# Attention and a routed expert layer on one core: GpSimd and SyncE put under a written order

## The chip, the cores and the metric

The kernel runs on one core of one Trainium2 chip. The metric is the device time of one execution in microseconds. TensorE (PE), VectorE (DVE), ScalarE (ACT), GpSimd (POOL) and SyncE (SP) each work through a queue of their own, in order; an instruction waits at the head of its queue until its semaphores are reached, and everything behind it waits with it. The program on every queue is fixed when the kernel is built.

## The reference

Softmax with one extra unit in the denominator, and then a layer of experts in which each token takes the one expert whose embedding is nearest in angle:

```python
scores = scale * q @ k.T                       # q, k, v: (8, 12, 448, 64)
m = scores.max(-1); e = exp(scores - m)
attn_out = (e / (e.sum(-1) + exp(-m) + 1e-9)) @ v
x = attn_out.transpose(0, 2, 1, 3).reshape(3584, 768)
logits = normed(x) @ normed(expert_emb).T / tau          # 8 experts
expert_idx = logits.argmax(1); gate_w = softmax(logits)[expert_idx]
out[mask_e] = gate_w * (relu(x[mask_e] @ w1[e]) @ w2[e]) # 768 -> 1024 -> 768
```

## The kernel before, in words

There are 8 batches. The 12 heads of a batch are taken in pairs, so a batch has `NP` = 6 groups, 48 in all, and each group has `NSLOT` = 8 slots. `pipeline` (L644) gives each step a position in slots, sorts the positions and runs the steps in that order. With `g` the group and 8g its first slot:

- `load_qk(n)` and `load_v(n)` (L156, L181) load queries, keys and values for two groups (g = 2n and 2n+1): nine and three DMAs, issued by SyncE, into three sets of buffers. A set is free once `front_q`, `front_k` (for q and k) or `front_v` and `sum_v` (for v) have used the loads three earlier.
- `front_q`, `front_k` transpose on TensorE. `front_v` (L250) is four GpSimd copies (L255 twice, L259, L263) that put v into one of two tiles `vab`; it must wait until TensorE has finished with the same tile two groups earlier.
- `scores` is a product on TensorE, an exponential on ScalarE and a subtraction of 1 on VectorE. `attend` and `attend_rest` (L302, L315) multiply by v and a column block of ones, so that the denominators come with the result; ScalarE copies it to `nb` and issues a small DMA of the denominators into `den`.
- `sum_v` (L194) adds up v over the rows in four GpSimd instructions (L198, L199, L202 twice), for the part of the sum that the subtraction of 1 took away; `sum_v_rows` (VectorE) and `sum_v_mm` (L218, TensorE, once a batch) finish it.
- `recip` (L337) makes reciprocals of the denominators on VectorE (tile `rc`, L346), and one GpSimd instruction (L348) spreads them into `rt`. `normalise` (L354) multiplies `rt` by a selection matrix on TensorE (L359) and then scales `nb` on VectorE (L364). There is one `rt` for two groups, so two `normalise` use each.
- The router of a batch (`router_mm` to `router_gate`) finds the expert of each token and the commonest expert of the batch. GpSimd takes a square root in it (L406), loads the number of the commonest expert into a register (L472) and fetches that expert's weights in seven pieces (`fetch`, `w_piece`, L485; three of w1, four of w2). `keep_xb` (L494) scatters the batch's x to DRAM by an indirect DMA from GpSimd (L503), which a later pass for the other experts reads if there are any.
- The expert's own work is cut into 15 chunks (`moe_chunks`, L557) that fill slots of the six groups from 6b+14 on: eight `moe_h`, then seven outputs y in the order (0,0), (0,1), the rest rows, (1,0), (1,1), (2,0), (2,1), at slots 1 and 5 of group 6b+17, 1, 5 and 7 of 6b+18, 1 and 5 of 6b+19. VectorE writes y into one of three tiles of the pool `yp`, and SyncE stores it (L568, L574). So the fourth y needs the store of the first to have landed, and the seventh, y(2,1), needs that of y(1,0).

What order the queues have: the pipeline is built under a manual schedule for TensorE alone, which keeps the order in which `pipeline` ran the steps. On the other engines the framework's scheduler orders the instructions at build time from its own estimates, held back in a few places by explicit "behind" edges. `fetch` holds one, behind the last `front_v`:

```python
    with tc.manual_schedule(engines={mybir.EngineType.PE}):
        pipeline(n)
```

Of the kernel before, what the change touches and what calls it, by code (L numbers as in the profile page):

```python
# [21 lines left out]
NP = H // 2  # L22
# [314 lines left out]
def recip(k, gg):  # L337

    nc = k.nc
    den, rc = k.den.pop(gg), k.rc[gg % 2]  # L340
    n = 2 * GP * CH
    i = nc.vector.tensor_scalar_add(den[:], den[:], float(S) + 1.0 + 1e-9)
    behind(k, i, k.last)
    nc.vector.reciprocal(out=den[:], in_=den[:])
    nc.vector.tensor_copy(out=rc[0:n, :], in_=den[:])
    nc.vector.tensor_tensor(out=rc[64 : 64 + n, :], in0=den[:], in1=rc[0:n, :].bitcast(F32), op=ALU.subtract)  # L346
    rt = k.rtp.tile([128, CH, CN], F32R, name="rt", tag="rt")
    nc.gpsimd.tensor_tensor(  # L348
        out=rt[:], in0=rc[:].bitcast(F32).unsqueeze(1).broadcast_to([128, CH, CN]), in1=k.chunk[:], op=ALU.mult
    )  # L350
    k.rts[gg] = rt
# [46 lines left out]
def router_tok(k, b):  # L398
# [7 lines left out]
    nc.gpsimd.tensor_tensor(out=nrm[:], in0=nrm[:], in1=k.half[:], op=ALU.pow)  # L406
# [12 lines left out]
    k.ohb[b], k.lg[b] = ohb, (l, nrm)  # L419

# [35 lines left out]
def router_pick(k, b):  # L456

    nc, p = k.nc, k.rp
    cp = k.work.tile([128, 512], F32, name="work", tag="work")
    nc.tensor.matmul(cp[:, 0 : 4 * E], lhsT=k.ones_b[:], rhs=k.ohb[b][:].rearrange("p t e -> p (t e)"),  # L460
                     start=True, stop=True)
    cnt = k.cnt_all[:, b, :]
    nc.vector.reduce_sum(out=cnt, in_=cp[:, 0 : 4 * E].rearrange("p (t e) -> p e t", e=E), axis=AX.X)
    mx = p.tile([128, 8], F32, name="mx", tag="mx")
    k.mx[b] = mx[:, 0:1]
    nc.vector.max(mx[:], cnt)
    nc.vector.max_index(k.idx_all[:, b, :], mx[:], cnt)
    idf = p.tile([128, 1], F32, name="idf", tag="idf")
    nc.vector.tensor_copy(out=idf[:], in_=k.idx_all[:, b, 0:1])
    oh0 = k.oh0_all[:, b, :]  # L470
    nc.vector.tensor_scalar(out=oh0, in0=k.iota[:], scalar1=idf[:, 0:1], scalar2=None, op0=ALU.is_equal)
    e0 = nc.values_load(k.idx_all[0:1, b, 0:1].bitcast(I32), engines=(mybir.EngineType.Pool,),  # L472
                        min_val=0, max_val=E - 1)
    k.e0[b], k.wts[b] = e0, ([], [])


def w_piece(k, e0, i):
# [7 lines left out]
    return w, k.nc.gpsimd.dma_start(w[:], src)  # L485


def fetch(k, b, i):
    w, inst = w_piece(k, k.e0[b], i)
    behind(k, inst, k.last_v)  # L490
    k.wts[b][i // 3 > 0].append(w)


def keep_xb(k, b):  # L494
# [7 lines left out]
    )  # L502
    nc.gpsimd.indirect_dma_start(  # L503
# [53 lines left out]
def moe_chunks(k, b):  # L557
# [21 lines left out]
def other_experts(k):  # L579
# [13 lines left out]
    with tc.If(any_ > 0):  # L593
# [6 lines left out]
        with tc.For_i(0, B * E, 1) as i:  # L600
# [3 lines left out]
            with tc.If(n > 0):  # L604
# [6 lines left out]
                w = [w_piece(k, e, j)[0] for j in range(7)]  # L611
# [32 lines left out]
def pipeline(k):  # L644
# [7 lines left out]
    put(3, lambda: build_late_consts(k))  # L652
    put(12, lambda: prep_expert_emb(k, k.emb, k.tau))
    put(5 * NSLOT, lambda: prep_expert_emb_t(k))
    for n in range(NG * B):
        put(max(-NSLOT, (n * GP - 6) * NSLOT + 4.5), lambda n=n: load_qk(k, n))
        put(max(-NSLOT, (n * GP - 6) * NSLOT + 7.5), lambda n=n: load_v(k, n))
        put(max(0, n * GP - 2) * NSLOT + 1.2, lambda n=n: sum_v(k, n))
        put(max(0, n * GP - 2) * NSLOT + 6.2, lambda n=n: sum_v_rows(k, n))
    for b in range(B):  # L660
        put((b * NP + 3) * NSLOT + 4.5, lambda b=b: sum_v_mm(k, b))
    for g in range(G):
# [3 lines left out]
        put(s - 1, lambda g=g: front_v(k, g))  # L666
# [37 lines left out]
def kernel(  # L704
# [86 lines left out]
```

## Time and profile before

| | before |
|---|---|
| median of 2 runs | 482.13 us (481.28 to 482.98) |
| the profiled execution | 485.81 us |
| its span, first to last instruction | 483.9 us |
| mean granted TensorE clock in it | 0.926 |

The span is what the engines' rows cover; the remaining 1.9 us of the profiled execution lie around it. The granted clock is a share of 2.4 GHz, and in a stretch it is either 1.0 or 0.5 (1.2 GHz). In the views below, times are microseconds from the start of the span unless ns is written; "x6" counts merged instructions; what stands in square brackets is the idle time of that engine just before, and what ended it.

### The profile page before, as it was taken

Reading aid. Unit: us, or ns where it says so; the run is one execution under the profiler, and the core shown is the slowest. Engines: PE = TensorE matmul, PEld = TensorE weight load, DVE = VectorE, ACT = ScalarE, POOL = GpSimd, SP = SyncE. Lnnn points to the kernel's source line nnn. Section 1 sums busy time; section 2 is a strip of 40 time slices with the busy share of each in tenths; the row PEclk is TensorE's granted clock in tenths of the full one; section 3 lists DMA queues with packets and bytes.
Section 4 is the critical chain, followed back from the end, with each engine's and each line's share of the span. In section 5 each row is a group of like instructions: output and inputs, shape, how many; then the busy total and the mean of one; then the engine's idle time right before and its main releaser. Section 6 shows DMA issues by size and latency. Waiting matters only on the chain.

```text
span 483.9 us, 7759 instructions
## 1 busy us (share of the span) xinstructions
PE 416.8 (86%) x2392; PEld 253.3 (52%) x2392; DVE 328.4 (68%) x827; ACT 274.5 (57%) x419; POOL 213.6 (44%) x412
## 2 busy tenths in 40 slices
PE   7587878877996979969898799969996999988986
PEld 5355545454564655636465454636564565654443
DVE  4458897948595666957669666867786686885213
ACT  2555776647684557836577456845785476824030
POOL 3764455446454435526245345545455353421400
PEclk9868999769998889979899899989999799999999
DMA  8762455559957786767978599577957572686893
GB/s 178 181 143 73 117 114 116 113 91 186 178 99 151 142 188 149 136 131 141 214 132 157 109 211 206 103 166 139 241 115 156 113 154 39 98 203 106 166 210 118
DMA packets 135373, 69.97 MB, mean 145 GB/s; under 512 B 101528, under 2 KB 129176, under 8 KB 135328
## 3 DMA queue, kind: packets, MB, share of 16 engines
q1 hardware_dynamic: 115392, 43.63, 36.8%
q0 software_dynamic: 16384, 25.17, 32.6%
q10 hardware_dynamic: 3552, 0.63, 0.9%
q8 instruction: 20, 0.33, 0.3%
q14 instruction: 25, 0.20, 0.1%
HBM read 83.39 MB, written 16.52 MB: 206 GB/s over the span
## 4 chain that ended last, share of the span: by engine, by line
PE 44%; DVE 16%; POOL 14%; issue 12%; DMA 6%; ACT 2%; POOLq 0%; SPq 0%; DVEq 0%; ACTq 0%
PE big L302 9%; PE work L515 8%; PE work L530 5%; DVE x L364 5%; DMA out_dram<-y 5%; PE big L277 5%; PE work L389 4%; DVE em L284 3%; PE work L545 3%; PE work L359 3%; POOL rt L348 3%; PE big L315 2%; POOL vs L202 2%; POOL vs L199 2%; PE work L231 2%
## 5 line engine op out<-in xcount | busy, mean ns | idle before, releaser
L282 ACT ACTIVATE e<-big 128x896 f32<-128x896 f32 x144 | 128.3, 921 | 65.3 <-DVE x L364 26.2
L284 DVE TENSOR_SCALAR em<-e 128x896 fp32r<-128x896 f32 x144 | 97.9, 680 | 39.0 <-ACT e L282 37.4
L255 POOL TENSOR_SCALAR vab<-vld 128x192 fp32r<-128x192 f32 x96 | 34.7, 374 | 139.2 <-PE big L302 109.9
L515 PE MATMUL work<-xb,w 128*128 128x448 bf16 x384 | 83.1, 356 | 3.7 <-DVE y L534 1.6
L364 DVE SCALAR_TENSOR_TENSOR x<-nb,sv,work 64x448 f32<-64x448 f32 x96 | 65.0, 677 | 28.3 <-PE work L359 25.9
L302 PE MATMUL big<-em,vab 128*128 128x448 f32 x288 | 77.4, 409 | 6.5 <-ACT e L282 5.5
L322 ACT COPY nb<-big 128x896 f32<-128x896 f32 x48 | 43.5, 907 | 61.0 <-PE big L315 60.9
L530 PE MATMUL work<-w,h 128*128 128x384 bf16 x384 | 68.7, 327 | 0.0
L302 PEld LDWEIGHTS big<-em,vab 128*128 128x128 f32 x288 | 59.0, 210 | 15.3 <-ACT e L282 7.5
L277 PE MATMUL big<-qt,kt 64*128 64x448 f32 x288 | 55.0, 434 | 5.4 <-ACT kt L246 2.4
L359 PE MATMUL work<-rt,sel 128*128 128x448 f32 x48 | 25.7, 535 | 38.7 <-POOL rt L348 30.2
L515 PEld LDWEIGHTS <-w 128*128 128x128 bf16 x384 | 35.1, 99 | 39.3 <-issue 12.0
L520 ACT ACTIVATE h<-work 128x448 bf16<-128x448 f32 x64 | 34.8, 544 | 33.8 <-PE work L515 33.6
L534 DVE TENSOR_SCALAR y<-work,g 128x384 f32<-128x384 f32 x48 | 29.2, 610 | 33.9 <-DMA out_dram<-y 16.2
L530 PEld LDWEIGHTS <-h 128*128 128x128 bf16 x384 | 35.9, 98 | 25.9 <-issue 5.3
L485 POOL DMA_DIRECT2D w<-in_moe_w_dram x56 | 43.4, 779 | 13.7 <-PE work L530 5.8
L234 DVE CAST qt<-work 128x448 fp32r<-128x448 f32 x48 | 29.9, 623 | 20.3 <-PE work L232 19.6
L277 PEld LDWEIGHTS big<-qt,kt 64*128 64x128 f32 x288 | 26.0, 205 | 20.4 <-issue 9.0
L359 PEld LDWEIGHTS work<-rt,sel 128*128 128x128 f32 x48 | 10.3, 214 | 49.2 <-POOL rt L348 35.9
L198 POOL TENSOR_TENSOR vs<-vld 128x256 f32<-128x256 f32 x24 | 18.1, 754 | 39.0 <-issue 33.2
L202 POOL TENSOR_TENSOR vs<-vs,vrest 64x128 f32<-64x128 f32 x48 | 26.6, 554 | 18.5 <-DMA xb_dram<-xb,keep_i 15.4
L246 ACT CAST kt<-work 128x512 fp32r<-128x512 f32 x48 | 28.2, 588 | 7.1 <-PE work L244 5.5
(117 smaller groups left out, 611.6 us busy)
## 6 DMA issues: line engine op xcount, KB each, us to landing
w<-in_moe_w_dram POOLq DMA_DIRECT2D x24, 512.0 KB, 6.9
w<-in_moe_w_dram POOLq DMA_DIRECT2D x32, 384.0 KB, 6.8
qm<-in_q_dram SPq DMA_DIRECT2D x72, 128.0 KB
vld<-in_v_dram SPq DMA_DIRECT2D x24, 384.0 KB
out_dram<-y SPq DMA_DIRECT2D x48, 192.0 KB
km<-in_k_dram SPq DMA_DIRECT2D x69, 128.0 KB
qrest<-in_q_dram SPq DMA_DIRECT2D x24, 64.0 KB
vrest<-in_v_dram SPq DMA_DIRECT2D x48, 32.0 KB
```

Of the source, the lines that this page charges most:

```text
L202: nc.gpsimd.tensor_tensor(out=vs[r, h::2, :], in0=vs[r, h::2, :], in1=t.vr[r, :, :], op=ALU.add)
L277: nc.tensor.matmul(ps[:, h, 0:S], lhsT=kt[64 * h : 64 * h + 64, 128 * j : 128 * j + 128], rhs=qt[64 * h : 64 * h + 64, :], start=True, sto ...
L282: k.last_e = nc.scalar.activation(e[:], ps[:, :, 0:S], ACT.Exp, scale=scale)
L284: k.last = nc.vector.tensor_scalar_sub(em[:], e[:], 1.0)
L302: nc.tensor.matmul(ps[:, h, 0:S], lhsT=va[:, j, 2 * h : 2 * h + 2, :], rhs=k.ems[g, j][:, h, :], start=(j == 0), stop=False,)
L322: nc.scalar.copy(out=nb[:, i, :, :], in_=ps[:, :, 0:S])
L359: nc.tensor.matmul(ps[:, 0:S], lhsT=k.sel[:, g % GP, :], rhs=rt[:].rearrange("p c n -> p (c n)"), start=True, stop=True)
L364: nc.vector.scalar_tensor_tensor(out=x[r, :], in0=nb[0:64, g % GP, h, :], scalar=k.sv[b][:, 2 * c + h : 2 * c + h + 1], in1=ps[r, 0:S], op ...
L485: return w, k.nc.gpsimd.dma_start(w[:], src)
L515: nc.tensor.matmul(ps[:, 0:S], lhsT=w1[c // 2][:, c % 2, 128 * f : 128 * f + 128], rhs=xb[:, c, :], start=(c == 0), stop=(c == NP - 1),)
L520: nc.scalar.activation(h[:], ps[:, 0:S], ACT.Relu)
L530: nc.tensor.matmul(ps[:, 0:SM], lhsT=hs[f][:, 128 * t : 128 * t + 128], rhs=w2[f // 2][:, f % 2, SM * n : SM * n + SM], start=(f == 0), st ...
```

## The change

GpSimd and SyncE join the manual schedule, so that their queues, too, run in the order of `pipeline`'s positions. With that, the steps are cut where they belong to different engines and get positions of their own:

- `recip` keeps the VectorE part; the spread of `rt` becomes `spread`, at slot 2 of the group whose slot 6.5 holds `normalise`.
- `front_v(g)` moves from slot 8g-1 to 8g-3.8. `sum_v` moves from slot 1.2 to 5 of its group; `sum_v_rows` from 6.2 to 8.
- `load_qk` moves from 4.5 to 5 and `load_v` from 7.5 to 7 of the same group.
- `fetch` moves from slot 7.7 to 4.3 of its group and loses its "behind" edge. `keep_xb` is cut: its two VectorE instructions (`keep_rows`) at `router_mm` + 13, the scatter at +16 instead of +14. The square root (`router_pow`) and the register load (`router_index`) are steps of their own at +5.6 and +11 (they ran with `router_tok` at +4 and `router_pick` at +7.6).
- The store of a y stands 2.5 slots behind its chunk.
- `build_late_consts` moves from 3 to 4.6. `prep_expert_emb`, whose position 12 is unchanged, holds one SyncE load (L129) and one GpSimd square root (L134).

```diff
@@ recip
+def spread(k, gg):
+    nc, rc = k.nc, k.rc[gg % 2]
     rt = k.rtp.tile([128, CH, CN], F32R, name="rt", tag="rt")
     nc.gpsimd.tensor_tensor(
...
@@ router_tok
-    nc.gpsimd.tensor_tensor(out=nrm[:], in0=nrm[:], in1=k.half[:], op=ALU.pow)
+def router_pow(k, b):
+    nrm = k.lg[b][1]
+    k.nc.gpsimd.tensor_tensor(out=nrm[:], in0=nrm[:], in1=k.half[:], op=ALU.pow)
@@ router_pick
+def router_index(k, b):
+    k.e0[b] = k.nc.values_load(k.idx_all[0:1, b, 0:1].bitcast(I32), engines=(mybir.EngineType.Pool,),
+                               min_val=0, max_val=E - 1)
+    k.wts[b] = ([], [])
@@ fetch
-    w, inst = w_piece(k, k.e0[b], i)
-    behind(k, inst, k.last_v)
+    w = w_piece(k, k.e0[b], i)
@@ moe_chunks
     def y(t, n):
         def run():
             yt = moe_y(k, hs, k.wts[b][1], k.g0[b], t, n)
-            nc.sync.dma_start(out_main(k.out, b * S, t, n), yt[:])
+            return lambda: nc.sync.dma_start(out_main(k.out, b * S, t, n), yt[:])
         return run
@@ pipeline
-    put(3, lambda: build_late_consts(k))
+    put(4.6, lambda: build_late_consts(k))
...
-        put(max(-NSLOT, (n * GP - 6) * NSLOT + 4.5), lambda n=n: load_qk(k, n))
-        put(max(-NSLOT, (n * GP - 6) * NSLOT + 7.5), lambda n=n: load_v(k, n))
-        put(max(0, n * GP - 2) * NSLOT + 1.2, lambda n=n: sum_v(k, n))
-        put(max(0, n * GP - 2) * NSLOT + 6.2, lambda n=n: sum_v_rows(k, n))
+        s = (n * GP - 6) * NSLOT
+        put(max(-NSLOT, s + 5), lambda n=n: load_qk(k, n))
+        put(max(-NSLOT, s + 7), lambda n=n: load_v(k, n))
+        s = max(n, n * GP - 2) * NSLOT if n < 2 else (n * GP - 2) * NSLOT
+        put(s + 5, lambda n=n: sum_v(k, n))
+        put(s + 8, lambda n=n: sum_v_rows(k, n))
...
-        put(s - 1, lambda g=g: front_v(k, g))
+        put(s - 3.8, lambda g=g: front_v(k, g))
...
             put(s + 2 * NSLOT + 0.5, lambda g=g: recip(k, g // GP))
+            put(s + 2 * NSLOT + 2, lambda g=g: spread(k, g // GP))
...
         put(s + 4, lambda b=b: router_tok(k, b))
+        put(s + 5.6, lambda b=b: router_pow(k, b))
         put(s + 7.6, lambda b=b: router_pick(k, b))
+        put(s + 11, lambda b=b: router_index(k, b))
         for i, o in enumerate((1, 2, 3, 4, 4, 5, 6)):
-            put(((b + 1) * NP + 3 + o) * NSLOT + 7.7, lambda b=b, i=i: fetch(k, b, i))
-        put(s + 14, lambda b=b: keep_xb(k, b))
+            put(((b + 1) * NP + 3 + o) * NSLOT + 4.3 + i / 100, lambda b=b, i=i: fetch(k, b, i))
+        put(s + 13, lambda b=b: keep_rows(k, b))
+        put(s + 16, lambda b=b: keep_xb(k, b))
...
+    def chunk(p, fn):
+        def run():
+            store = fn()
+            if store:
+                put(p + 2.5, store)
+        put(p, run)
...
-            put(p, fn)
-    for slot in sorted(at):
-        for fn in at[slot]:
+            chunk(p, fn)
+    while at:
+        for fn in at.pop(min(at)):
             fn()
...
-    with tc.manual_schedule(engines={mybir.EngineType.PE}):
+    with tc.manual_schedule(engines={mybir.EngineType.PE, mybir.EngineType.Pool, mybir.EngineType.SP}):
         pipeline(n)
```

## Rows read from the trace of the kernel before

**Rows 1.** The page: busy time, share of the span and instructions of each engine.

```profile
PE 416.8 (86%) x2392; PEld 253.3 (52%) x2392; DVE 328.4 (68%) x827; ACT 274.5 (57%) x419; POOL 213.6 (44%) x412
```

**Rows 2.** Waits of TensorE from 125 to 420: waiter, releaser, us in total, times, longest.

```profile
PE work L359 <- POOL rt L348: 22.3, 6, 4.7
PE work L359 <- DVE y L534: 5.6, 3, 2.5
```

**Rows 3.** Timeline of GpSimd, 140.9 to 155: start, length, engine, line, operation.

```profile
141.56 0.79 POOL L485 DMA_DIRECT2D w<-in_moe_w_dram  x1
143.98 0.73 POOL L198 TENSOR_TENSOR vs<-vld 128x256 f32<-128x256 f32 x1 [1.64 <-issue]
144.90 1.07 POOL L503 DMA_INDIRECT xb_dram<-xb,keep_i  x1 [0.18 <-issue]
...
147.14 0.73 POOL L202 TENSOR_TENSOR vs<-vs,vrest 64x128 f32<-64x128 f32 x1
150.85 0.45 POOL L202 TENSOR_TENSOR vs<-vs,vrest 64x128 f32<-64x128 f32 x1 [2.98 <-DMA xb_dram<-xb,keep_i]
...
152.74 0.82 POOL L485 DMA_DIRECT2D w<-in_moe_w_dram  x1 [0.15 <-issue]
153.63 1.02 POOL L348 TENSOR_TENSOR rt<-rc,chunk 128x448 fp32r<-128x448 f32 x1
```

**Rows 4.** Timelines of VectorE (148 to 149) and TensorE (150 to 155).

```profile
148.61 0.18 DVE L346 TENSOR_TENSOR rc<-den,rc 56x32 fp32r<-56x32 f32 x1
...
154.71 0.74 PE L359 MATMUL work<-rt,sel 128*128 128x448 f32 x1 [4.26 <-POOL rt L348]
```

**Rows 5.** Stretches at clock 0.5, length and busy sums: behind five L348 waits; behind two y waits.

```profile
sum 27.40, PE 23.68 PEld 13.07 DVE 17.79 ACT 10.59 POOL 3.44; mean PE 4.74 PEld 2.61 DVE 3.56 ACT 2.12 POOL 0.69
...
sum 6.60, PE 6.55 PEld 4.58 DVE 6.43 ACT 4.43 POOL 2.05; mean PE 3.27 PEld 2.29 DVE 3.21 ACT 2.22 POOL 1.02
```

**Rows 6.** Waits of TensorE, 95 to 120; two stretches at 0.5 behind them, summed.

```profile
PE work L359 <- POOL rt L348: 5.0, 2, 2.7
...
sum 10.20, PE 10.20 PEld 6.34 DVE 7.62 ACT 5.57 POOL 1.87; mean PE 5.10 PEld 3.17 DVE 3.81 ACT 2.79 POOL 0.93
```

**Rows 7.** Timeline of SyncE 160 to 178; last, TensorE 172 to 178.

```profile
162.20 1.51 SPq L172 DMA_DIRECT2D qm<-in_q_dram  x3
...
170.90 1.01 SPq L568 DMA_DIRECT2D out_dram<-y  x2
172.00 0.44 SPq L186 DMA_DIRECT2D vld<-in_v_dram  x1
172.54 1.82 SPq L188 DMA_DIRECT2D vrest<-in_v_dram  x2
...
177.05 0.74 PE L359 MATMUL work<-rt,sel 128*128 128x448 f32 x1 [2.49 <-DVE y L534]
```

**Rows 8.** The chain that ended last, 160 to 180: start, length, what.

```profile
162.50 7.08 DMA den<-nb
...
170.90 5.38 DMA out_dram<-y
```

**Rows 9.** Timelines of the start: SyncE, ScalarE, GpSimd, TensorE, VectorE.

```profile
29.74 0.53 SPq L129 DMA_DIRECT2D emb_raw<-in_moe_expert_emb_dram  x1
...
36.71 0.83 ACT L132 ACTIVATE emb_sq<-emb_raw 8x768 f32<-8x768 f32 x1
...
24.81 0.67 POOL L255 TENSOR_SCALAR vab<-vld 128x192 fp32r<-128x192 f32 x2
...
39.16 0.58 POOL L134 TENSOR_TENSOR emb_nrm<-emb_ss,half 8x1 f32<-8x1 f32 x1
...
36.16 1.47 PE L302 MATMUL big<-em,vab 128*128 128x448 f32 x6 [0.68 <-POOL vs L199]
...
39.10 0.30 PE L218 MATMUL work<-vst,ind 128*128 128x24 f32 x2
...
17.82 0.29 DVE L100 CAST sel<-sel_f 128x256 fp32r<-128x256 f32 x1 [2.67 <-POOL sel_f L97]
```

More of the change, by code (lines that the diff above doesn't have):

```diff
@@ L262, in front_v @@
     )
-    k.last_v = nc.gpsimd.tensor_scalar(
+    nc.gpsimd.tensor_scalar(
         out=va[64:128, 3, 2, :], in0=t.vr[64:128, i, :],
@@ L471, in router_pick @@
     nc.vector.tensor_scalar(out=oh0, in0=k.iota[:], scalar1=idf[:, 0:1], scalar2=None, op0=ALU.is_equal)
-    e0 = nc.values_load(k.idx_all[0:1, b, 0:1].bitcast(I32), engines=(mybir.EngineType.Pool,),
-                        min_val=0, max_val=E - 1)
-    k.e0[b], k.wts[b] = e0, ([], [])
+def router_index(k, b):
+    k.e0[b] = k.nc.values_load(k.idx_all[0:1, b, 0:1].bitcast(I32), engines=(mybir.EngineType.Pool,),
+                               min_val=0, max_val=E - 1)
+    k.wts[b] = ([], [])
 def w_piece(k, e0, i):
@@ L484, in w_piece, with keep_rows @@
         src = k.w2[bass.ds(e0, 1), :, :].rearrange("o (f p) m -> p (o f) m", p=128)[:, 2 * i - 6 : 2 * i - 4, :]
-    return w, k.nc.gpsimd.dma_start(w[:], src)
+    k.nc.gpsimd.dma_start(w[:], src)
+    return w
 def fetch(k, b, i):
-    w, inst = w_piece(k, k.e0[b], i)
-    behind(k, inst, k.last_v)
+    w = w_piece(k, k.e0[b], i)
     k.wts[b][i // 3 > 0].append(w)
-def keep_xb(k, b):
+def keep_rows(k, b):
     nc = k.nc
@@ L502, in keep_xb @@
     )
+    k.keep[b] = idx
+def keep_xb(k, b):
+    nc, idx = k.nc, k.keep[b]
     nc.gpsimd.indirect_dma_start(
@@ L572, in yr, with store @@
         yt = moe_yr(k, hs, k.wts[b][1], k.g0[b])
-        for n in range(2):
-            nc.sync.dma_start(k.out[b * S + SM : b * S + S, SM * n : SM * n + SM], yt[64 * n : 64 * n + 64, :])
+        def store():
+            for n in range(2):
+                nc.sync.dma_start(k.out[b * S + SM : b * S + S, SM * n : SM * n + SM], yt[64 * n : 64 * n + 64, :])
+        return store
     return [h(f) for f in range(NF)] + [y(0, 0), y(0, 1), yr, y(1, 0), y(1, 1), y(2, 0), y(2, 1)]
@@ L610, in other_experts @@
                 nc.vector.tensor_copy(out=g[64:128, 3:4], in_=g[0:64, 3:4])
-                w = [w_piece(k, e, j)[0] for j in range(7)]
+                w = [w_piece(k, e, j) for j in range(7)]
                 w1, w2 = w[:3], w[3:]
@@ L750 @@
     n.ld, n.qts, n.kts, n.ems, n.nbs, n.den, n.va, n.sv = {}, {}, {}, {}, {}, {}, {}, {}
-    n.mx, n.lg, n.e0, n.xb, n.xs, n.ohb, n.g0, n.wts, n.avs, n.rts = {}, {}, {}, {}, {}, {}, {}, {}, {}, {}
+    n.keep, n.mx, n.lg, n.e0, n.xb, n.xs, n.ohb, n.g0, n.wts, n.avs, n.rts = {}, {}, {}, {}, {}, {}, {}, {}, {}, {}, {}
     n.emb, n.tau = moe_expert_emb, moe_tau
-    with tc.manual_schedule(engines={mybir.EngineType.PE}):
+    with tc.manual_schedule(engines={mybir.EngineType.PE, mybir.EngineType.Pool, mybir.EngineType.SP}):
         pipeline(n)
```

## The prediction

> **What bounds the kernel now.** I read the page first: TensorE is busy for 86% of the span and no other engine for more than 68% [rows 1], so the time is TensorE's work plus what it waits for plus what a halved clock adds. Next the waits of TensorE in the regular part, 125 to 420. Two matter: `normalise` (L359) waits 22.3 us in six pieces for the spread of `rt` on GpSimd, and 5.6 us in three for VectorE's y [rows 2]. Then the timelines around one of each.
>
> The spread. Its input `rc` is ready at 148.61 + 0.18 = 148.8, yet GpSimd starts it at 153.63, and TensorE, there since 150.45, goes on at 154.71 [rows 3, 4]. In between GpSimd does what the scheduler put in front. The scatter is issued at 144.90 inside a `sum_v`; the last L202 of that `sum_v` idles 2.98 us until 150.85 on the scatter's landing; four copies of `front_v` and a fetch (0.82) follow [rows 3]. So 4.26 us of the 4.84 us delay reach TensorE. The pattern comes once a batch, five times in this stretch (the sixth piece of the six is small).
>
> The y. y(2,1) needs the tile that y(1,0) left. The store of y(1,0) stands on SyncE behind the load of q and k that begins at 162.20; it is issued at 170.90 and lands 5.38 later [rows 7, 8]. VectorE stands at y(2,1) till then, and TensorE waits 2.49 us [rows 7].
>
> The clock. Behind five of the spread waits it is at 0.5 for 27.4 us together, of which TensorE is busy 23.7; behind two y waits 6.6 us, busy 6.55 [rows 5]. Work at half speed loses half its length: 11.8 us and 3.3 us.
>
> **The change part by part.** Sums are made against the profiled execution, 485.81 us, which is 3.7 us above the median of 482.13; I carry the difference over to the median.
>
> The spread is now written at slot 2, right behind the scatter (slot 7.9 of the group before) and ahead of `front_v` (4.2) and the fetch (4.3). From the end of `front_v` at about 141.4, GpSimd's queue is fetch 0.79, four instructions of `sum_v` at about 0.73 [rows 3], together 2.9, the scatter 1.07: done at about 146.2, before `rc` at 148.8. The 1.64 us idle ahead of L198 [rows 3] is a wait for the one `vs` tile and should go, since `sum_v_rows` now stands well before the next `sum_v`. The spread runs from 148.9 to 150.0, and TensorE comes at 150.45: no wait. I take all of the 22.3 us [rows 2] and 11.8 us of clock [rows 5]. The other end: if the spread too is held until the scatter lands, 5.9 us after its issue (144.90 to 150.85 [rows 3]), it ends at 145.1 + 5.9 + 1.1 = 152.1 and 1.7 us of each of five waits stays, 8.5 us, with half the clock loss.
>
> Two earlier waits of this kind add 5.0 us, with 10.2 us at half clock behind them [rows 6]. In the second `rc` itself is late, so I keep 1 us of wait and 1 us of clock loss: gain 4.0 + 4.1 = 8.1. Together the gains are 42.2 us.
>
> The stores. `load_v` (slot 7) now comes before the store of y(1,0) (5 + 2.5 = 7.5). In the rows its three DMAs take from 172.00 to 174.36, 2.4 us, and stand behind that store [rows 7]. Moved ahead, the store is issued at about 173.2, lands at 178.6 with the 5.38 of [rows 8], and L359 follows 0.7 later at 179.3. TensorE is there at 177.05 - 2.49 = 174.56, so it waits 4.8 us instead of 2.49. This holds for the four batches whose outputs meet loads (the loads end before the fifth). I take 4.6 us each: 18.4 against 5.6 now [rows 2], a cost of 12.8. A wait of this length brought 11.8/5 = 2.4 us of clock loss in the spread's case; four times that, 9.6, less the 3.3 there now, is 6.3. The ends: a landing as short as 2 us makes the wait 1.4, below today's; the den DMA's 7.08 [rows 8] in place of 5.38 makes it 6.5.
> y(0,0) and y(0,1) are stored right behind loads in both orders, but TensorE comes to y(1,0) about 7 us earlier once the spread's wait is gone, about when they land. I put 2 us in all; it can be nothing or 3 us in each of five batches.
>
> The start. `prep_expert_emb` stays at slot 12, now in SyncE's and GpSimd's written order. Its square root (L134, run at 39.16) needs the load issued at 29.74 and the square on ScalarE at 36.71, and now stands ahead of `front_v(2)` (12.2), which ran at 24.81 [rows 9]. Behind it queue `front_v(2)`, `sum_v(1)`, `front_v(3)`, `sum_v(2)`; `attend(2)` (36.16) needs the first, and L218 (39.10) the last, through VectorE [rows 9]. If the load lands near 32 and ScalarE squares at once, the root ends near 34, and 1.3 + 2.8 + 1.3 + 2.8 + 1 bring L218 to about 43, a loss of 4; if ScalarE keeps 36.71, 8. The constants, run in one piece, spare VectorE's 2.67 us at L100 [rows 9], but `attend(2)` takes that back. I take 4, with ends 0 and 8.
>
> Parts at nothing. `front_v` earlier: it waits for TensorE to release `vab` in any position. The fetches were already behind `front_v`; the last w2 fetch of a pair may wait for y(2,1)'s product, and behind it stands only a `front_v` that is needed a group later. The root of the router comes behind a fetch, 0.8 us later; the chain after it has a group to spare. `keep_rows` keeps its two short instructions. The order on VectorE and ScalarE is still the scheduler's and may shift with the rest: bad for as much as L100's 2.67 us once [rows 9], or good for as much.
>
> Sum: 42.2 - 12.8 - 6.3 - 2 - 4 = 17.1 gained; 485.8 - 17.1 = 468.7, and against the median 465.
>
> **Rivals.**
> *Stores land fast.* With y(1,0) landing 2 us after issue, the y wait is no worse than now. Then the 42.2 us less the start's 4 is 38, 444 to 447. For it: nothing but that store would be late. Against: 5.38 in the row, and a denser DMA load when the batch gets shorter.
> *The gain is moved, not made.* The spread still waits for the scatter (8.5 us and 6 us of clock stay), the start costs 8, and the y waits are as forecast: 42.2 - 14.5 - 12.8 - 6.3 - 2 - 8 = -1.4; half of these give 474 to 484. For it: the landing wait sits on a plain copy that reads nothing the scatter writes, so it may follow GpSimd's queue anywhere.
> *Slower: SyncE's order becomes the bound.* The y tiles come back only behind twelve load DMAs. If loading q and k takes 11 us instead of 8.7, because two loads now follow each other closer, and the landing 7.08 [rows 8], the y wait is 4.8 + 2.3 + 1.7 = 8.8, with 2.4 of clock 11.2 per batch, 45 in four (8.9 now); the same landing makes y(1,0) wait 3 us in five batches, 15, with 12 of clock. Then 42.2 - 36 - 27 - 8 = -29 at the worst; with one half of the second part and the start at 4, about -11: 493. It decides from about 10 us of y wait, clock included, per batch.
> The Trainium skill (DMA: Bandwidth & Descriptors, "Queues, rings and completion order") says that each DMA engine consumes the descriptors of one issuing queue in ring order. By it a store behind `load_v` also waits for that load's data, an estimate of 448 KB more on the ring, so the y wait would lie nearer this rival than the forecast; no row here shows a y store directly behind a value load with its landing.
>
> **How the numbers follow.** Forecast 0.46, its own range 456 to 474; stores land fast 0.20; moved 0.17; slower 0.17. Two per cent, about what a measurement of this kernel can tell from no change, is 472.5 to 491.8. Faster: 0.40 of the forecast's 0.46 and all of the second, 0.60. Same: the forecast's rest and the third, 0.23. Slower: 0.17. The range leaves out half of the best case and half of the worst: 445 to 491.
>
> **What would show it.** Right: L359's wait for L348 nearly gone from 125 to 420; L348 starting within 0.2 us of `rc`; four waits of L359 for y of 4 to 6 us, with SyncE's rows in the order q, k, v, y; `attend(2)` and L218 not before 36 and 41. Wrong: a spread that still starts 3 us behind `rc`; y waits below 2 us (then near 445) or above 8 (then above 482); or a new wait of VectorE in its own changed order.

## Result: 465.16 us, and the profile after

The changed kernel takes 465.16 us (median of 2 runs, 464.83 to 465.49) against 482.13: a ratio of 0.965, 95% interval 0.957 to 0.973. It is faster, and the forecast of 465.0 is met. The sections below show that two of its terms were each about 11 to 14 us too large, with opposite signs. Medians and ratios, here and below, leave out the executions in a slower state that some runs had.

Line numbers move: the spread is L353 (L348 before), `normalise`'s product L364 (L359) and its scaling L369 (L364), y L552 (L534), its store L586 (L568), a weight piece L497 (L485), the scatter L521 (L503). The profiled execution took 465.49 us, its span is 464.0, the mean granted clock 0.952. The page of the changed kernel, busy time and two of its costliest groups (busy, mean ns of one, idle before and what ended it); the first line answers to [rows 1]:

```profile
PE 407.0 (88%) x2392; PEld 247.2 (53%) x2392; DVE 332.3 (72%) x827; ACT 276.8 (60%) x419; POOL 222.7 (48%) x412
...
L353 POOL TENSOR_TENSOR rt<-rc,chunk 128x448 fp32r<-128x448 f32 x24 | 24.8, 1035 | 110.7 <-DVE rc L346 110.6
...
L552 DVE TENSOR_SCALAR y<-work,g 128x384 f32<-128x384 f32 x48 | 29.1, 608 | 38.7 <-DMA out_dram<-y 21.2
```

GpSimd now stands at the spread, 110.7 us in all, and what ends that is its input `rc`: the spread no longer comes late, it is early. VectorE's y waits 21.2 us for stores. The waits of TensorE from 125 to 420, to be laid beside [rows 2]:

```profile
PE work L287 <- DVE x L369: 6.1, 3, 2.2
PE work L231 <- DVE y L552: 5.4, 4, 3.3
PE work L364 <- POOL vab L259: 4.5, 5, 0.9
PE work L364 <- POOL rt L353: 2.5, 1, 2.5
```

The 22.3 us for `rt` are 2.5, once, near the end. The y wait has moved from `normalise` to the next transposes (L231) and scores (L287), because the scheduler placed y(2,1) elsewhere on VectorE: 11.5 us against 5.6. Five waits of 0.9 us are new. The first of them, on GpSimd, VectorE and TensorE (start, length; answers to [rows 3, 4]):

```profile
144.50 1.34 POOL L521 DMA_INDIRECT xb_dram<-xb,keep_i  x1 [1.36 <-DVE emx L291]
147.35 1.04 POOL L353 TENSOR_TENSOR rt<-rc,chunk 128x448 fp32r<-128x448 f32 x1 [1.51 <-DVE rc L346]
...
147.07 0.19 DVE L346 TENSOR_TENSOR rc<-den,rc 56x32 fp32r<-56x32 f32 x1
...
148.57 0.61 DVE L234 CAST qt<-work 128x448 fp32r<-128x448 f32 x1
...
149.33 0.44 PE L364 MATMUL work<-rt,sel 128*128 128x448 f32 x1 [0.89 <-POOL vab L259]
```

The spread starts at 147.35, 0.09 after `rc` at 147.07 + 0.19. TensorE still goes on only 0.94 us after the spread's end; the view names a copy of v as what ended that, and the run "three" below shows that it is VectorE's copy of q (L234, done at 149.18).

TensorE's work is the same in all kernels here, so its time can be cut at two marks: the start of `attend(14)` and of `attend(47)`. In between lies the steady part. Two stretches of the changed kernel, the steady part and the end, with TensorE's busy time, then PEld, DVE, ACT, POOL, granted clock, DMA share, GB/s:

```profile
129.00:403.67 274.67, 256.25 (x1561) 156.65 (x1560) 221.47 (x552) 185.86 (x284) 145.92 (x256) 0.99 0.78 156
403.67:464.00 60.33, 49.79 (x296) 26.08 (x294) 22.38 (x64) 12.46 (x23) 11.05 (x14) 0.97 0.75 162
```

The same cut of each run's profile, in us; idle is the stretch less TensorE's busy time (waits). A higher busy time for the same instructions is mostly the halved clock, not all of it: in the five kernels whose steady part has a granted clock of 1.00 (GpSimd alone, value load behind, stores first, both edits, three edits) it still runs from 251.2 to 254.0. So differences of 3 us in this column are not the clock's for certain.

| kernel | span | to attend(14) | steady: length | busy | idle | after attend(47) |
|---|---|---|---|---|---|---|
| before | 483.9 | 131.1 | 294.9 | 264.7 | 30.2 | 57.9 |
| changed | 464.0 | 129.0 | 274.7 | 256.3 | 18.4 | 60.3 |
| GpSimd alone | 456.5 | 128.0 | 268.1 | 253.6 | 14.5 | 60.4 |
| SyncE alone | 502.3 | 138.5 | 305.2 | 263.2 | 42.1 | 58.5 |
| value load behind | 453.9 | 127.3 | 267.2 | 254.0 | 13.3 | 59.4 |
| stores first | 447.1 | 128.5 | 258.0 | 251.4 | 6.6 | 60.6 |
| weights later | 461.3 | 126.8 | 274.1 | 256.6 | 17.5 | 60.4 |
| root late | 456.9 | 120.9 | 276.9 | 256.0 | 20.9 | 59.1 |
| spread back | 501.4 | 135.5 | 306.5 | 268.4 | 38.1 | 59.4 |
| spread back, scatter after | 483.6 | 131.5 | 288.8 | 264.6 | 24.2 | 63.2 |
| both edits | 442.9 | 122.6 | 259.4 | 251.2 | 8.1 | 61.0 |
| three edits | 439.2 | 121.0 | 257.9 | 251.6 | 6.3 | 60.3 |

From before to changed: start -2.1, steady part -20.2 (11.8 of idle, 8.4 of busy time), end +2.4. That is where the 19.9 us of span went.

### The profile page after: what moved, and what is told of

The parts are those of the page before. It is cut to its first block, busy times and chain, and to the rows that moved or that the text cites. A ratio compares the mean times of both kernels' runs of the same rounds, so it can differ in the third digit from the quotient of the medians.

```text
span 464.0 us, 7798 instructions
## 1 busy us (share of the span) xinstructions
PE 407.0 (88%) x2392; PEld 247.2 (53%) x2392; DVE 332.3 (72%) x827; ACT 276.8 (60%) x419; POOL 222.7 (48%) x412
## 4 chain that ended last, share of the span: by engine, by line
PE 42%; DVE 22%; POOL 17%; DMA 7%; issue 7%; ACT 3%; SPq 0%; POOLq 0%; ACTq 0%; DVEq 0%
PE work L533 9%; PE big L302 7%; DVE em L284 6%; PE work L548 6%; PE big L277 4%; PE work L394 4%; DMA out_dram<-y 4%; DVE x L369 4%; POOL vs L202 3%; POOL vab L255 3%; ACT e L282 3%; DVE y L552 2%; POOL vs L199 2%; PE work L563 2%; POOL rt L353 2%
## 5 line engine op out<-in xcount | busy, mean ns | idle before, releaser
L284 DVE TENSOR_SCALAR em<-e 128x896 fp32r<-128x896 f32 x144 | 105.1, 730 | 28.3 <-ACT e L282 27.5
L533 PE MATMUL work<-xb,w 128*128 128x448 bf16 x384 | 85.4, 363 | 3.5 <-DVE y L552 1.8
L302 PE MATMUL big<-em,vab 128*128 128x448 f32 x288 | 72.9, 390 | 11.5 <-ACT e L282 7.6
L353 POOL TENSOR_TENSOR rt<-rc,chunk 128x448 fp32r<-128x448 f32 x24 | 24.8, 1035 | 110.7 <-DVE rc L346 110.6
L369 DVE SCALAR_TENSOR_TENSOR x<-nb,sv,work 64x448 f32<-64x448 f32 x96 | 64.9, 676 | 4.4 <-PE work L364 2.3
L302 PEld LDWEIGHTS big<-em,vab 128*128 128x128 f32 x288 | 54.8, 197 | 19.8 <-POOL vs L202 5.4
L255 POOL TENSOR_SCALAR vab<-vld 128x192 fp32r<-128x192 f32 x96 | 37.9, 409 | 45.0 <-PE big L302 23.6
L538 ACT ACTIVATE h<-work 128x448 bf16<-128x448 f32 x64 | 34.8, 544 | 38.2 <-PE work L533 38.1
L533 PEld LDWEIGHTS <-w 128*128 128x128 bf16 x384 | 36.0, 101 | 40.5 <-issue 14.5
L277 PE MATMUL big<-qt,kt 64*128 64x448 f32 x288 | 52.8, 417 | 5.3 <-ACT kt L246 2.3
L552 DVE TENSOR_SCALAR y<-work,g 128x384 f32<-128x384 f32 x48 | 29.1, 608 | 38.7 <-DMA out_dram<-y 21.2
L497 POOL DMA_DIRECT2D w<-in_moe_w_dram x56 | 43.4, 777 | 14.8 <-PE work L548 5.5
L382 ACT ACTIVATE xs<-x 128x448 f32<-128x448 f32 x48 | 27.8, 578 | 19.5 <-DVE x L369 19.4
L234 DVE CAST qt<-work 128x448 fp32r<-128x448 f32 x48 | 29.8, 622 | 8.7 <-PE work L232 7.8
L289 ACT ACTIVATE e<-work 128x448 f32<-128x448 f32 x48 | 26.1, 545 | 10.7 <-PE work L287 10.6
L231 PE MATMUL work<-ident,qm 128*128 128x128 f32 x144 | 27.7, 304 | 5.4 <-DVE y L552 5.4
## 6 DMA issues: line engine op xcount, KB each, us to landing
qm<-in_q_dram SPq DMA_DIRECT2D x72, 128.0 KB
km<-in_k_dram SPq DMA_DIRECT2D x69, 128.0 KB
```

Of the source, the lines that this page charges most:

```text
L255: nc.gpsimd.tensor_scalar(out=va[:, 0:3, 2 * h, :], in0=t.v[:, 2 * i + h, :, :], scalar1=1.0, scalar2=0.0, op0=ALU.mult, op1=ALU.add,)
L277: nc.tensor.matmul(ps[:, h, 0:S], lhsT=kt[64 * h : 64 * h + 64, 128 * j : 128 * j + 128], rhs=qt[64 * h : 64 * h + 64, :], start=True, sto ...
L284: k.last = nc.vector.tensor_scalar_sub(em[:], e[:], 1.0)
L302: nc.tensor.matmul(ps[:, h, 0:S], lhsT=va[:, j, 2 * h : 2 * h + 2, :], rhs=k.ems[g, j][:, h, :], start=(j == 0), stop=False,)
L369: nc.vector.scalar_tensor_tensor(out=x[r, :], in0=nb[0:64, g % GP, h, :], scalar=k.sv[b][:, 2 * c + h : 2 * c + h + 1], in1=ps[r, 0:S], op ...
L533: nc.tensor.matmul(ps[:, 0:S], lhsT=w1[c // 2][:, c % 2, 128 * f : 128 * f + 128], rhs=xb[:, c, :], start=(c == 0), stop=(c == NP - 1),)
```

## The experiments

Each ratio is to the kernel before, on the same chip, with its 95% interval; the changed kernel's is 0.965 (0.957 to 0.973).

**The two halves, each alone.** GpSimd in the written order, SyncE left as before:

```diff
-    with tc.manual_schedule(engines={mybir.EngineType.PE, mybir.EngineType.Pool, mybir.EngineType.SP}):
+    with tc.manual_schedule(engines={mybir.EngineType.PE, mybir.EngineType.Pool}):
-        put(max(-NSLOT, s + 5), lambda n=n: load_qk(k, n))
-        put(max(-NSLOT, s + 7), lambda n=n: load_v(k, n))
+        put(max(-NSLOT, s + 4.5), lambda n=n: load_qk(k, n))
+        put(max(-NSLOT, s + 7.5), lambda n=n: load_v(k, n))
-                put(p + 2.5, store)
+                store()
```

> GpSimd keeps the written order of the change; SyncE goes back to the scheduler, with its loads at slots 4.5 and 7.5 and each store beside its chunk, which gives the order of stores and loads of the kernel before. Theory by the forecast's sizes: SyncE's part costs 12.8 + 6.3 + 2 = 21.1 us, so without it the kernel takes about 444. Theory by the waits seen after the change: TensorE loses about 11 us at y (3.3 + 2.8 + 3.3 + 1.7) against 5.6 before, and little clock, so SyncE's part costs 5 to 9 and this takes 456 to 460. Rival, SyncE's order costs nothing because VectorE's backlog ends the same stretch anyway: 464 to 466.

Measured: 459.33 us, ratio 0.947 (0.939 to 0.955). Within the second theory's range: SyncE's part of the change costs some 6 us (by the spans 464.0 - 456.5 = 7.5), not 21. GpSimd's part is worth 27.4 us of span, not 38. The waits of TensorE from 125 to 420 in this run tell why:

```profile
PE work L364 <- POOL vab L259: 4.5, 5, 0.9
PE work L533 <- DVE qt L234: 4.0, 4, 1.0
PE work L364 <- DVE y L552: 3.0, 3, 1.5
PE work L364 <- POOL rt L353: 2.4, 1, 2.4
PE work L287 <- DVE x L369: 1.4, 4, 0.4
```

Without the spread's wait, TensorE meets VectorE 16 times, 4.5 + 4.0 + 3.0 + 1.4 = 12.9 us. (The first line belongs to VectorE too, see "three".) The kernel before has, beside the 5.6 of [rows 2], two short pieces of the same kind, 6.6 us in all:

```profile
PE work L515 <- DVE qt L234: 0.6, 1, 0.6
PE work L287 <- DVE x L364: 0.4, 1, 0.4
```

SyncE in the written order, with the kernel before for all else:

```diff
-    with tc.manual_schedule(engines={mybir.EngineType.PE}):
+    with tc.manual_schedule(engines={mybir.EngineType.PE, mybir.EngineType.SP}):
-        put(max(-NSLOT, (n * GP - 6) * NSLOT + 4.5), lambda n=n: load_qk(k, n))
-        put(max(-NSLOT, (n * GP - 6) * NSLOT + 7.5), lambda n=n: load_v(k, n))
+        put(max(-NSLOT, (n * GP - 6) * NSLOT + 5), lambda n=n: load_qk(k, n))
+        put(max(-NSLOT, (n * GP - 6) * NSLOT + 7), lambda n=n: load_v(k, n))
...
+                put(p + 2.5, store)
```

> The kernel before, with SyncE alone put under the written order (loads at slots 5 and 7, stores 2.5 slots behind their chunks); GpSimd stays with the scheduler. Theory by the forecast's sizes: 482 + 21 = 503. Theory by the waits seen after the change: 487 to 491, with y(1,0)'s store behind the value load and waits for y of 2 to 4 us in four batches beside the spread's 22 us. Rival, SyncE's order costs nothing: 480 to 484.

Measured: 504.82 us, ratio 1.042 (1.033 to 1.051). The number is the first theory's, and the reason is not. The waits of TensorE from 125 to 420 hold none for y:

```profile
PE work L515 <- DMA w<-in_moe_w_dram: 37.6, 5, 8.9
PE work L359 <- POOL rt L348: 11.2, 5, 2.7
```

and on GpSimd and TensorE, around the first of the five (176.56 to 185.49):

```profile
177.64 0.67 POOL L255 TENSOR_SCALAR vab<-vld 128x192 fp32r<-128x192 f32 x2 [3.51 <-DMA vld<-in_v_dram]
...
178.97 2.47 POOL L485 DMA_DIRECT2D w<-in_moe_w_dram  x3
...
185.49 0.93 PE L515 MATMUL work<-xb,w 128*128 128x448 bf16 x2 [8.93 <-DMA w<-in_moe_w_dram]
```

With SyncE's order fixed, the scheduler rearranged GpSimd's: three weight pieces went together behind copies that stood waiting for a load of v, and the expert's first product waits for them. This run measures no y wait; it shows only that SyncE's half does harm when GpSimd's order is not written too.

**The spread's place.** The spread alone put back behind the copies and the fetch:

```diff
-            put(s + 2 * NSLOT + 2, lambda g=g: spread(k, g // GP))
+            put(s + 2 * NSLOT + 4.5, lambda g=g: spread(k, g // GP))
```

> The changed kernel with the spread alone put back to slot 4.5 of its group, behind the copies of v and the fetch (slots 4.2 and 4.3). Theory: in the five batches with a scatter the spread again starts some 3 us behind its input; by the rows of the changed kernel it would end at about 151.6 instead of 148.4 in the first, so TensorE waits 2.4 us longer in each, and a half clock of some 2 us follows it: 5 times 2.4 to 4.4, 477 to 487. By the forecast's sizes (22.3 + 11.8 us all given back): 499. Rival, the gain came from the rest of GpSimd's order and the spread's place is worth little: under 468.

Measured: 502.81 us, ratio 1.037 (1.029 to 1.045): 37.6 us above the changed kernel, close to the 34 that the forecast gave the spread's waits and clock together, and slower than before. In the steady part idle rises by 19.7 and busy by 12.1 (22.3 and 11.8 in the forecast); another 6.5 fall at the start. The rival is out. The first such place, on GpSimd, then VectorE and TensorE:

```profile
151.64 1.33 POOL L521 DMA_INDIRECT xb_dram<-xb,keep_i  x1 [1.37 <-DVE emx L291]
...
155.74 0.24 POOL L263 TENSOR_SCALAR vab<-vrest 64x64 fp32r<-64x64 f32 x1 [1.58 <-PE work L287]
...
157.22 1.02 POOL L353 TENSOR_TENSOR rt<-rc,chunk 128x448 fp32r<-128x448 f32 x1
...
154.36 0.18 DVE L346 TENSOR_TENSOR rc<-den,rc 56x32 fp32r<-56x32 f32 x1
...
158.30 0.47 PE L364 MATMUL work<-rt,sel 128*128 128x448 f32 x1 [2.74 <-POOL rt L353]
```

The spread starts 2.7 us after `rc`, behind a copy that idled 1.58 and a fetch. Here the view names a product as what ended that idling; in three of the five places behind a scatter it names the scatter's landing (waits of GpSimd, 125 to 420):

```profile
POOL vab L263 <- DMA xb_dram<-xb,keep_i: 5.7, 3, 2.6
```

The same with the scatter moved behind the spread:

```diff
-        put(s + 16, lambda b=b: keep_xb(k, b))
+        put(s + 21, lambda b=b: keep_xb(k, b))
```

> As the kernel with the spread back at slot 4.5, but the scatter goes behind it, to slot 4.9 of the same group (it was at 7.9 of the group before). Theory, the scatter's landing holds the last copies of v, and through the queue the spread: without it the spread starts about 1.5 us behind its input instead of 3, and the time comes down to 468 to 474. Rival, what delays the spread there is the queue itself (the copies, which wait for TensorE, and the fetch): no better than the kernel with the scatter in front, within 2 us.

Measured: 484.18 us, ratio 0.998 (0.991 to 1.004). 18 us come back, and in the waits of TensorE from 125 to 420 the line L364 <- L353 falls from 21.6 us to 3.0. Of the 21.6, 14.6 lay in the five places behind a scatter, and these are all gone: there the scatter's landing, waited for by a copy in front of the spread, was the cause. The other 7.0, where copies and two fetches alone stood in front, became the 3.0 that remain: that is the queue's own share. But 484.2 is not the 468 to 474 expected: the scatter now holds the copies of the group behind it, and TensorE has a new wait (L315 <- DVE emx, 7.0 us). How the one leads to the other, and what the rest of the time goes to, is not shown. The spread's place alone wasn't enough, nor the scatter's; of the orders tried the changed kernel has the one in which the landing holds nothing that TensorE needs soon. On GpSimd, later in this run:

```profile
151.96 1.47 POOL L521 DMA_INDIRECT xb_dram<-xb,keep_i  x1 [0.19 <-issue]
...
158.30 0.24 POOL L263 TENSOR_SCALAR vab<-vrest 64x64 fp32r<-64x64 f32 x1 [1.48 <-DMA xb_dram<-xb,keep_i]
```

**The stores.** First the value load alone behind the store of y(1,0), then all loads behind it:

```diff
-        put(max(-NSLOT, s + 7), lambda n=n: load_v(k, n))
+        put(max(-NSLOT, s + 7.6), lambda n=n: load_v(k, n))
```

> The changed kernel with the load of v alone moved from slot 7 to 7.6, so that the store of y(1,0) goes ahead of its three DMAs, and still behind the nine of q and k. Theory by the forecast's step (the three DMAs take 2.4 us of issue and the store lands as long after its issue as before): VectorE's waits of 5.4, 2.7, 3.3 and 2.3 us fall by 2.0 to 2.4 each, TensorE gets 5 to 8 us back, 457 to 460. Rival, landings on SyncE's ring follow each other, so that the store is held by the loads of q and k whatever stands between: waits within 0.7 us of now, 463 to 466. Second rival, all of the y wait goes as with the stores first: below 453.

Measured: 456.63 us, ratio 0.946 (0.938 to 0.955), just under the first theory's range, and the same ratio as with SyncE left to the scheduler (0.947): within the noise, the place of this one load is the whole difference between SyncE's two orders. In the chain that ended last, the stores of y(1,0) of the changed kernel and where they lie (start, length to landing):

```profile
166.33 4.99 DMA out_dram<-y
...
219.02 2.32 DMA out_dram<-y
...
268.99 3.78 DMA out_dram<-y
...
320.85 2.38 DMA out_dram<-y
```

and in this run three of the four, with no value load in front:

```profile
162.78 2.15 DMA out_dram<-y
...
261.13 2.45 DMA out_dram<-y
312.01 2.14 DMA out_dram<-y
```

The landings are 2.8, 1.3 and 0.2 us shorter, and the load's own 2.0 us of issue (164.31 to 166.33 on SyncE in the first) no longer stand in front. But the load's data is not the only thing that moved. GpSimd issues two weight pieces near each of these stores; at the first, in the changed kernel and in this run:

```profile
166.13 1.51 POOL L497 DMA_DIRECT2D w<-in_moe_w_dram  x2
...
164.23 1.51 POOL L497 DMA_DIRECT2D w<-in_moe_w_dram  x2
```

So they come 0.2 us ahead of the store there and 1.5 us behind it here; at the third store they come 0.7 us behind it there, and 2.6 us here, when it has landed. Only at the fourth do they come behind the store in both (by 0.3 and 0.7 us), and there the load in front makes 0.2 us of landing.

```diff
-        put(max(-NSLOT, s + 5), lambda n=n: load_qk(k, n))
-        put(max(-NSLOT, s + 7), lambda n=n: load_v(k, n))
+        put(max(-NSLOT, s + 7.6), lambda n=n: load_qk(k, n))
+        put(max(-NSLOT, s + 7.7), lambda n=n: load_v(k, n))
```

> The changed kernel with the loads of q, k and v 2.6 and 0.7 slots later (slots 7.6 and 7.7), so that the stores of y(0,1), of the rest rows and of y(1,0) all go ahead of the twelve loads. Theory: VectorE's waits for y(1,0)'s store (5.4, 2.7, 3.3, 2.3 us in the changed kernel) go, TensorE gets its 11 us back, less a little of VectorE's own backlog: 453 to 457. Rival, the y wait only covers VectorE's backlog, and the matmul of the next scores waits for x instead: 462 to 466. Second rival, the later loads come late to the transposes: above 466.

Measured: 449.77 us, ratio 0.928 (0.921 to 0.936), below the theory's range: 15.4 us under the changed kernel and 9.6 under the run with SyncE as before. The store goes out at once, and the steady part runs at full clock with 6.6 us of idle in 258:

```profile
128.45:386.48 258.03, 251.40 (x1561) 155.49 (x1560) 220.36 (x552) 185.75 (x284) 148.41 (x256) 1.00 0.83 167
```

Of the 16.6 us that the steady part gains, 11.8 are idle and 4.9 are busy time (3.3 of it by the two half-clock stretches below). So some 15 us is what the late stores cost in the changed kernel, clock and VectorE's backlog included; with SyncE as before it was 9.6. TensorE's waits for VectorE of that run are gone too, all but the 4.5 us of "POOL vab": 4.0 + 3.0 + 1.4 = 8.4 us. The two kernels differ in SyncE's order alone, so VectorE's lateness there comes from that order.

**The weights.** Does a weight piece in flight hold SyncE's loads, and through them the store?

```diff
-            put(((b + 1) * NP + 3 + o) * NSLOT + 4.3 + i / 100, lambda b=b, i=i: fetch(k, b, i))
+            put(((b + 1) * NP + 3 + o) * NSLOT + 7.7 + i / 100, lambda b=b, i=i: fetch(k, b, i))
```

> The changed kernel with the weight pieces fetched at slot 7.7 of their groups, as before the change, instead of 4.3; all else as changed. In the changed kernel a piece of 384 KB is issued about 1.1 us ahead of the first q load, whose first part completes only 4.8 us after its issue, and the issue of the fifth load then takes 2.8 to 3.0 us. Theory, the piece in flight holds the loads up and through SyncE's queue the store of y(1,0): with the piece behind them that stall is under 1.5 us, the store goes out 1.5 to 3 us earlier and TensorE gets 4 to 8 us back, 457 to 461. Rival, the stall is the six loads' own: no difference, 463 to 467. Second rival, the pieces now come late to their products: above 467.

Measured: 464.04 us, ratio 0.961 (0.954 to 0.968): no difference clear of the noise. The store of y(1,0) is issued 6.7 to 7.8 us after y is made (5.9 to 6.8 in the changed kernel), and three of the four land later after their issue:

```profile
162.85 6.45 DMA out_dram<-y
...
216.75 4.93 DMA out_dram<-y
...
267.51 3.05 DMA out_dram<-y
...
318.54 4.74 DMA out_dram<-y
```

The theory as I wrote it falls: the store does not go out earlier. But a piece in flight may still matter, by the landing and not by the loads. On GpSimd, at the first of these stores:

```profile
162.17 1.48 POOL L497 DMA_DIRECT2D w<-in_moe_w_dram  x2
```

Here two pieces are issued 0.7, 1.0, 0.2 and 1.0 us ahead of the four stores, which land in 6.45, 4.93, 3.05 and 4.74; in the changed kernel 0.2 and 0.1 us ahead of the first two and behind the others (4.99, 2.32, 3.78, 2.38). All the stores of y that stand in the chain that ended last, in the traces of all these kernels, fit that: with pieces issued 0.4 to 3 us ahead the landing took 4.7 to 7.7 us, whether a value load stood directly in front or not; with pieces behind, or 8 us ahead, 2.1 to 3.8 and once 5.1; within 0.3 us ahead, 2.3 to 5.0. The 5.38 that the forecast went by is of the first kind, with no value load in front; on GpSimd, before, 0.9 us ahead of the store at 170.90:

```profile
170.03 0.78 POOL L485 DMA_DIRECT2D w<-in_moe_w_dram  x1
```

No run moved the pieces alone to a place behind the stores, so this is a pattern over many landings and not a cause shown.

**The start.** `prep_expert_emb` cut in two:

```diff
+    k.emb_sb, k.emb_ss = emb, ss
+
+
+def prep_expert_emb_norm(k, tau):
+    nc, emb, ss = k.nc, k.emb_sb, k.emb_ss
...
     put(12, lambda: prep_expert_emb(k, k.emb, k.tau))
+    put(22, lambda: prep_expert_emb_norm(k, k.tau))
```

In the changed kernel, on ScalarE, GpSimd and TensorE (answers to [rows 9]):

```profile
34.00 0.83 ACT L132 ACTIVATE emb_sq<-emb_raw 8x768 f32<-8x768 f32 x1
...
35.00 0.58 POOL L134 TENSOR_TENSOR emb_nrm<-emb_ss,half 8x1 f32<-8x1 f32 x1 [13.83 <-DMA km<-in_k_dram]
...
35.97 2.61 PE L302 MATMUL big<-em,vab 128*128 128x448 f32 x6 [3.20 <-POOL vab L255]
45.08 0.62 PE L218 MATMUL work<-vst,ind 128*128 128x24 f32 x2 [3.56 <-DVE vst L211]
```

GpSimd stands 13.83 us at the root. (The releaser named is a load of keys, which the root doesn't read; the square on ScalarE ends at 34.83, just before.) Behind it queue the copies for `attend(2)` and the sums for L218.

> The changed kernel with the square root of the expert embedding (and the three VectorE operations behind it) at slot 22 instead of 12, behind the third sum of v; its load and ScalarE's square stay at slot 12. Theory: GpSimd's 13.8 us of idling ahead of that root held up the copies of v and the sums behind it; TensorE's waits of 3.2 us at attend(2) and 3.6 us at the sum over v go: 458 to 461. Rival, the start is bound by what the copies need anyway (v loads, ScalarE): the waits return elsewhere within the first two batches, 463 to 466.

Measured: 459.9 us, ratio 0.950 (0.941 to 0.958). `attend(14)` begins at 120.9 instead of 129.0, so the root cost 8.1 us there. 2.2 of it go again in the steady part, in longer y waits. On GpSimd and TensorE (L139 is the root, L223 the product):

```profile
34.94 0.58 POOL L139 TENSOR_TENSOR emb_nrm<-emb_ss,half 8x1 f32<-8x1 f32 x1 [3.14 <-ACT emb_sq L132]
...
35.43 0.30 PE L223 MATMUL work<-vst,ind 128*128 128x24 f32 x2
```

The root runs at the same time, but nothing stands behind it: the product that was at 45.08 is at 35.43.

**Both, and a third edit.** Loads behind the stores and the root late:

> The changed kernel with both edits: loads at slots 7.6 and 7.7, behind the stores, and the root of the expert embedding at slot 22. With the root late alone, attend(14) began 8.1 us earlier, and the y waits later gave 2.2 of it back; with the stores first there are no y waits. Theory: the two add up, 449.8 less 8: 440 to 443. Rival, the shorter start only brings the loads closer together and costs a new wait in the steady part: 444 to 449.

Measured: 443.73 us, ratio 0.913 (0.904 to 0.923), between the two ranges. By the spans (442.9 against 447.1) 4.2 of the 8 us add up; to `attend(14)` 1.6 us of the root's gain are missing, and the steady part loses 1.3. With the router's gate later as well:

```diff
-        put(s + 18, lambda b=b: router_gate(k, b))
+        put(s + 23, lambda b=b: router_gate(k, b))
```

> The kernel with both edits and the router's gate (eight short VectorE instructions) 5 slots later, at slot 6.9 instead of 1.9 of its group. Five times TensorE idles 0.86 us ahead of a normalise that the trace puts down to a GpSimd copy; the spread had ended 0.94 us before. Theory: it is VectorE, which frees the PSUM tile with its copy of q late, behind the gate; with the gate later these five go: 4 us less than both edits, 436 to 439. Rival, it is GpSimd as the trace says: no change against both edits, within 1.5 us.

Measured: 441.67 us, ratio 0.911 (0.904 to 0.919). The edit touches VectorE only, and the five waits of 0.9 us for "POOL vab" are gone from the view. At the first place (GpSimd, then TensorE; L369 is `normalise` here):

```profile
139.28 1.03 POOL L358 TENSOR_TENSOR rt<-rc,chunk 128x448 fp32r<-128x448 f32 x1 [1.43 <-DVE rc L351]
...
140.37 0.47 PE L369 MATMUL work<-rt,sel 128*128 128x448 f32 x1
```

`normalise` now follows the spread by 0.06 us. So it was VectorE, whose copy of q stood behind the gate. The time is not the 436 to 439 expected: the gain over both edits is unclear by the intervals, and the waits for ScalarE's copy of k grow from 1.5 us to 3.1. This version is the best of the study, 8.9% under the kernel before and 5% under the changed one.

**The changed kernel again**, beside the last three runs:

> The changed kernel itself once more, beside these. Both theories: 463 to 467, and the same waits for y on VectorE of 5.4, 2.7, 3.3 and 2.3 us to within 2 us each.

Measured: 467.28 us, ratio 0.970 (0.961 to 0.979), at the upper end of the expected range; the ratio agrees with the first. The y waits on VectorE were 7.3, 2.1, 3.1 and 2.3 us: their size in the first batch varies by 2 us from run to run.

## Why the prediction was right, step by step, and where it was not

**What bounds the kernel.** Right: TensorE's work plus waits plus the halved clock. In the steady part these were 251.4 us at full clock ("stores first"), 13.3 more of busy time (the half-clock stretches of [rows 5] make 15.1) and 30.2 of idle before.

**The spread, 22.3 + 11.8.** The mechanism is shown. It starts 0.09 us after `rc`; put back, it costs 37.6 us; and the scatter's landing is what made it late. The clock term was about right: with GpSimd alone the steady part has no half-clock stretch left, where before they made 11.8 us behind the spread's waits and 3.3 behind the y's; busy time falls by 11.1. The wait term was too large: idle falls by 15.7, not 22.3. The failing step is "TensorE comes at 150.45: no wait", in which only GpSimd stood against TensorE. VectorE was next, with 12.9 us against 6.6: 6.3 more, about the 6.6 that are missing. Of the 12.9, 4.5 are at that very `normalise`, where VectorE's copy of q stands behind the router's gate ("three"); the other 8.4 go when the stores go first.

**The two earlier waits, 8.1.** From 95 to 120 the wait for `rt` falls from 5.0 to 0.9 us, 4.1 against the 4.0 forecast. Two half-clock stretches of 3.4 us remain there instead of 10.2 together: a gain of about 1.7, not 4.1.

**The y store, 12.8 + 6.3.** The order on SyncE was right, and that VectorE stands at y(2,1); the size was not. The forecast looked for four waits of 4 to 6 us at `normalise`; they came at the transposes and scores, 3.3, 2.8, 3.4 and 2.0 us. That is 11.5 us, not 18.4, of which 5.6 were there before. The working took one landing, 5.38, for four batches; it was 4.99, 2.32, 3.78 and 2.38. The 5.38 was a store with a weight piece issued just ahead of it (see "The weights"), and the forecast did not ask what else was in flight. The clock term failed more: two half-clock stretches follow the y waits, not four. Their rows, summed:

```profile
sum 6.80, PE 6.59 PEld 3.37 DVE 5.12 ACT 3.75 POOL 0.90; mean PE 3.29 PEld 1.68 DVE 2.56 ACT 1.88 POOL 0.45
```

Half of 6.59 is 3.3, not 9.6; and 3.3 was lost at y before. So SyncE's half cost 6.6 us in the steady part (3.9 of idle, 2.7 of busy time) instead of 21.1. The step that a 2 to 5 us wait always brings 2.4 us of clock was drawn from the spread's waits of 4.2 to 4.7 us, and the shorter y waits did not bear it out. **y(0,0), y(0,1), 2:** VectorE waited for neither in the steady part: nothing, the lower end.

**The start, 4.** The mechanism is shown, and the root's place was mis-sized by half: it costs 8.1 us up to `attend(14)`, the upper end, and L218 came at 45.08 where the forecast had about 43. The forecast let ScalarE square "at once" near 32; the square runs at 34.00, behind ScalarE's own work. Against the kernel before, the start is 2.1 us shorter; with the 5.8 of the two earlier waits taken out it is 3.7 longer, so the 4 was met only because other parts of the start, not looked into, gave back about as much.

**The end, 0.** 2.4 us, not foreseen, and no run tested its cause. The trace shows where they are: 7 us behind the start of `attend(47)` the fifth y of a batch waits 2.47 us on VectorE for a store (1.07 before), `rc` and the spread follow it, and TensorE waits 2.46 us for `rt` (1.28 before); 1.6 of the 2.4 are busy time, at a mean granted clock of 0.97 where it was 1.00.

**The sum.** -38.2 became -27.4 for GpSimd's half and +21.1 became +7.5 for SyncE's: -17.1 forecast, -19.9 measured in the spans. That the time came out to within 0.2 us is luck: two terms, one sized without VectorE and one from a single landing, were too large together, with opposite signs.

**Rivals.** "Stores land fast" (444 to 447) was half true: two of four landed in 2.3 us, but the store's late issue remained. "Moved, not made" is out. "SyncE's order becomes the bound" is out for this change; without GpSimd's half, SyncE's does make the kernel slower, by late weights.

The Trainium skill (DMA: Bandwidth & Descriptors, "Queues, rings and completion order") says that a queue's descriptors are consumed in ring order. The runs agree in direction and show little of a price: taking the value load away gives landings of 2.14 to 2.45, but where the weight pieces stand behind the store in both kernels the difference is 0.2 us; the 2.8 and 1.3 us of the other two landings have pieces in another place as well.

## What to carry to other kernels

When a wait is taken from the bounding engine, price what that engine meets next: look for the engine that was hidden by the wait (here VectorE) and subtract its waits before the gain is booked. One landing is not a price: look at several, and at what else was in flight at each. On an in-order queue, put what a reused buffer waits for (a store) ahead of loads that have slack, and put an instruction whose input comes from far (a root behind a load and another engine) behind everything that is ready. A forecast that meets the total is not confirmed by it: the halves, run alone, showed two errors that cancelled, and one run that hit its number by another mechanism.

## What was not expected of the hardware

- A small copy on GpSimd (L263, 64 partitions) waits for the landing of an indirect DMA that writes nothing it reads: 1.48 us with the scatter behind the spread, as 2.98 us at L202 in [rows 3]. Why, and whether it is the chip or the way the program was built that asks for it, is open.
- Where SyncE has stores alone, a store still lands slowly when weight pieces go out just ahead of it. In the chain of the changed kernel, near its end, with two pieces issued at 437.67 on GpSimd:

```profile
438.05 6.01 DMA out_dram<-y
```

- The name behind a wait can be wrong: the five waits put down to a GpSimd copy went when VectorE's order alone was changed.
